# First attention units without zeros in their loads: keys between zeros that lie on chip, eight buffers instead of four

## The chip, the cores and the metric

One Trainium2 chip, and of it one core. A core has five engines that run their own instruction streams and wait for each other by semaphores: PE (matrix products, with a queue of its own for weight loads, PEld), DVE (vector work), ACT (activations and copies), POOL (vector work on SBUF alone) and SP, which in this kernel issues almost all transfers between memory and SBUF. Sixteen DMA engines carry the transfers out. The metric is the time of one execution in microseconds (us), the median over runs.

## The reference

Attention in chunks of 32 queries, each of which sees 8 memory keys and a window of the sequence (16 keys to the left, its own 32, 8 to the right), and then a layer of two matrix products with a leaky bend between them:

```python
batch, n_heads, seq, head_dim = (4, 8, 768, 64)
chunk, left_ctx, right_ctx = (32, 16, 8)
...
    k_full = np.concatenate([mem_k, k_ctx], axis=2)
    v_full = np.concatenate([mem_v, v_ctx], axis=2)
    scores = scale * np.matmul(q_c, k_full.transpose(0, 1, 3, 2))
    scores = scores - np.max(scores, axis=-1, keepdims=True)
    a = np.exp(scores)
    a = a / (np.sum(a, axis=-1, keepdims=True) + 1e-09)
    out[:, :, c_start:c_end] = np.matmul(a, v_full)
...
h = x @ w_in                                          # 3072 x 512 by 512 x 2048
g = np.maximum(h, 0.0) + alpha * np.minimum(h, 0.0)
return (g @ w_out)                                    # 2048 x 512
```

All is 32-bit floating point. The two weight matrices reach the kernel as 64-bit words and are decoded on the chip into a high and a low part, so that each product of the layer is three products in PE's faster 32-bit form.

## The kernel before

The attention is cut into 32 units: half a sequence (384 queries) of a pair of heads. Four units (the four pairs of a half) give one block of 384 columns of the layer's input. The layer runs over blocks and over 16 slices `f` of the hidden width: `up` (L723) makes `h_ps` from the input's high and low parts (`xh`, `xl`) and `w_in`, ACT and DVE bend it (L732, L735) and split it, `down` (L753) adds it up in `o_ps` with `w_out`.

The first eight units (`NWIN`, two blocks) go another way than the later 24, since PE has nothing else to do until their results are there. A unit of this kind is loaded by `load_first` (L486) into a buffer `early` that borrows the place of a weight slice: `NSET` = 4 such buffers, in the places of the last four slices. It holds queries, keys and values of a pair of heads. The 128 rows of queries and keys are 64 of one head and 64 of the other. So that one product over all 128 rows gives the scores of both heads apart, the queries come from memory with zeros: for each chunk of 32 queries 64 columns, 32 with the first head's rows filled and 32 with the second's. That is `NQ` = 768 columns for 384 queries, and 656 KB for queries and keys. The values, 256 KB, come in a second load.

`windows` (L496) then runs a unit through this chain:
- PE: `score_products` (L300), twelve products of 64 weight columns by 64 keys (L312). Before those of the first three units stand `stir` products (L298) of the tile `busy`, whose result nobody uses, 8, 2 and 2 of them (`STIR`).
- DVE: `top` (L505 or L507 hide keys outside the sequence, L509 takes the maximum), `less` (L513); ACT: `exps` (L517); DVE: `total` (L521), `inverse` (L524); POOL: `scale` (L534, L538) into `ew`, spread so that a transpose puts every key in its own row.
- PE: `turn` (L546, six transposes); ACT: `keep` (L551, two copies); PE: `values` (L559); ACT and DVE: `split` (L474, L477) into `xh` and `xl`.

Two buffers each serve the scores in PSUM, `e`, `ew` and the turned weights. A weight slice passes through ACT and DVE too (`decode_part`: L622, L630, L634, L638, L646, L649).

The order of all engines is written by a planner, `Plan`: each step has an engine, an assumed cost, what it reads and writes and when it is due. It fills the engines as a list scheduler would, with the step that has the longest way behind it first; `SHIFT` corrects that number for single steps, and `LAND` is the time it assumes from the end of a load's sending to its landing. The instructions then stand in that order in each engine's stream, and each engine runs its stream strictly in order. SP too: a load that must wait for its buffer holds up every load behind it.

Of the kernel before, what the change touches and what calls it, by code (L numbers as in the profile page):

```python
# [72 lines left out]
HOP, LAND, FOLLOW = 0.07, 2.3, 0.1  # L73
# [29 lines left out]
STIR = (8, 2, 0, 0)  # L103
# [78 lines left out]
def body(ctx: ExitStack, tc: tile.TileContext, qvw, kw, first, w_in, w_out, alpha, out):  # L182
# [22 lines left out]
    nc.vector.memset(busy, 1.0)  # L205
# [94 lines left out]
    def score_products(u):  # L300
# [6 lines left out]
        q = t[:, :NQ].rearrange("p (c x) -> p c x", c=NT * NJ)  # L307
        keys = t[:, NQ:NQ + NT * NKT].rearrange("p (t k) -> p t k", t=NT)
        for n in range(2 * NJ):
            for i in range(2):  # L310
                t, j = n // NJ * 2 + i, n % NJ
                nc.tensor.matmul(  # L312
                    out=st["s"][i * 2 * CH:(i + 1) * 2 * CH, n],
                    lhsT=q[:, t * NJ + j],
                    rhs=keys[:, t, STARTS_WIN[j]:STARTS_WIN[j] + KW],
                    start=True, stop=True,
                )
# [167 lines left out]
    def load_first(u):  # L485
        blk, pr = divmod(u, NPAIR)  # L486
        t = early[u % NSET]

        def load(lo, hi):
            nc.sync.dma_start(out=t[:, lo:hi], in_=first[blk, pr, :, lo:hi])  # L490
# [4 lines left out]

    def windows(u):  # L496
# [5 lines left out]
        def top():  # L502
            s = st["s"]
            if u // NPAIR % 2 == 0:
                nc.vector.memset(s[0:2 * CH, 0, 0:LEFT], NEG)  # L505
            else:
                nc.vector.memset(s[2 * CH:4 * CH, 2 * NJ - 1, KW - NM - RIGHT:KW - NM], NEG)  # L507
# [450 lines left out]
```

## Time and profile before

| | us |
|---|---|
| median of three runs | 598.39 (598.30 to 599.01) |
| the profiled execution | 598.74 |
| its span, first to last instruction | 596.8 |
| PE busy | 588.1 (99%) |
| DVE busy | 387.1 (65%) |
| ACT busy | 210.9 (35%) |
| POOL busy | 37.9 (6%) |
| DMA engines, mean busy share in the first ten of 40 slices | 0.8, 0.9 or more three times, 0.6, 0, 0, 0.2, 0.2, 0.2 |

The granted TensorE clock is 1.00 throughout. In an order of time a row gives the start and the duration in us, the engine, the line of the kernel, the operation, output<-input with their shapes, the count, and in brackets how long the engine had stood idle and for whom. In a table of groups the two numbers behind the bar are busy us and mean ns of one, then the idle us before them. `SPq` is SP's stream of transfers. In a table of waits the three numbers are us in total, times, and the longest.

### The profile page before, as it was taken

To read this page: it belongs to the slowest core of one execution; us is meant where nothing else is said; L and a number is where in the kernel's file an instruction comes from. 1 tells how busy PE (TensorE), PEld (TensorE's weight loads), DVE (VectorE), ACT (ScalarE), POOL (GpSimd) and SP (SyncE) were. 2 spreads that over 40 slices of the span, in tenths; PEclk is the share of its full clock that TensorE was granted. 3 is DMA by queue.
4 is the path that set the end of the run, shared out by engine and by line. 5 is a ranking of instruction groups with operands and counts; after the bars stand their busy time and mean duration, and the time that the engine had idled before them with its cause. 6 is when DMAs were issued, how large, how long until landed. Compare 5 with 4: busy or idle time off the path is not lost.

```text
span 596.8 us, 10948 instructions
## 1 busy us (share of the span) xinstructions
PE 588.1 (99%) x4412; PEld 504.9 (85%) x4412; DVE 387.1 (65%) x904; ACT 210.9 (35%) x580; POOL 37.9 (6%) x61
## 2 busy tenths in 40 slices
PE   7999999999999999999999999999999999999997
PEld 4789989888998989989898888888888888888886
DVE  5888889887958768695895852861862771530530
ACT  3788887635122504423233302302400411210201
POOL 3510000010001101010010100100100100000000
PEclk9999999999999999999999999999999999999999
DMA  8999600222040312503304003003101000000001
GB/s 328 351 400 407 246 0 1 66 65 89 2 153 2 100 33 69 152 3 100 100 1 154 1 1 100 2 0 112 60 1 36 0 1 36 36 1 0 1 1 70
DMA packets 21075, 48.95 MB, mean 82 GB/s; under 512 B 2464, under 2 KB 5792, under 8 KB 21024
## 3 DMA queue, kind: packets, MB, share of 16 engines
q1 hardware_dynamic: 20880, 48.12, 22.8%
q8 instruction: 34, 0.56, 0.4%
q14 instruction: 17, 0.14, 0.1%
q10 hardware_dynamic: 144, 0.13, 0.1%
HBM read 41.95 MB, written 6.29 MB: 81 GB/s over the span
## 4 chain that ended last, share of the span: by engine, by line
PE 96%; DMA 3%; SPq 0%; ACT 0%; issue 0%; ACTq 0%
PE h_ps L723 45%; PE o_ps L753 44%; PE a_ps L438 3%; DMA early<-first 3%; PE s_ps L337 2%; PE a_ps L559 1%; PE o_ps L546 0%; PE s_ps L312 0%; SPq L490 0%; SPq L599 0%; ACT o_t L810 0%; ACTq L810 0%
## 5 line engine op out<-in xcount | busy, mean ns | idle before, releaser
L723 PE MATMUL h_ps<-xh,w 128*128 128x384 f32 (+1 forms) x896 | 248.7, 358 | 0.0
L723 PEld LDWEIGHTS h_ps<-xh,w 128*128 128x128 f32 x896 | 164.9, 188 | 16.0
L753 PE MATMUL o_ps<-w,gh 128*128 128x512 f32 x528 | 162.7, 389 | 0.0
L723 PE MATMUL h_ps<-xl,w 128*128 128x384 f32 (+1 forms) x448 | 162.6, 363 | 0.0
L732 ACT ACTIVATE g<-h_ps 128x384 f32<-128x384 f32 (+1 forms) x112 | 60.4, 540 | 195.3 <-PE h_ps L723 129.8
L735 DVE SCALAR_TENSOR_TENSOR g<-g,rise,h_ps 128x384 f32<-128x384 f32 (+1 forms) x112 | 74.7, 668 | 74.8 <-ACT g L732 74.1
L753 PEld LDWEIGHTS o_ps<-w,gh 128*128 128x128 f32 x528 | 99.1, 188 | 20.5
L413 DVE STREAM_TRANSPOSE pt<-e 32x64 f32<-32x64 f32 (+1 forms) x336 | 99.3, 300 | 7.4 <-POOL e L392 2.0
L753 PE MATMUL o_ps<-w,gl 128*128 128x512 f32 x264 | 102.8, 389 | 0.0
L723 PEld LDWEIGHTS h_ps<-xl,w 128*128 128x128 f32 x448 | 84.1, 188 | 10.2
L753 PE MATMUL o_ps<-w,xh 128*128 128x512 f32 x240 | 74.8, 393 | 0.0
L753 PEld LDWEIGHTS o_ps<-w,gl 128*128 128x128 f32 x264 | 49.6, 188 | 10.2
L477 DVE TENSOR_TENSOR xl<-a_ps,xh 128x384 fp32r<-128x384 f32 x32 | 17.6, 552 | 59.7 <-ACT xh L474 59.0
L753 PEld LDWEIGHTS o_ps<-w,xh 128*128 128x128 f32 x240 | 45.0, 188 | 8.9
L392 POOL TENSOR_TENSOR e<-e,den 128x384 f32<-128x384 f32 x24 | 22.8, 948 | 419.6 <-DVE den L389 270.0
L474 ACT CAST xh<-a_ps 128x384 fp32r<-128x384 f32 x32 | 15.0, 482 | 95.5 <-PE a_ps L438 93.7
L741 DVE CAST gh<-g 128x512 fp32r<-128x512 f32 (+1 forms) x72 | 28.8, 401 | 30.6 <-PE o_ps L753 28.2
L745 DVE TENSOR_TENSOR gl<-g,gh 128x512 fp32r<-128x512 f32 (+1 forms) x72 | 46.6, 648 | 1.7
L371 ACT ACTIVATE e<-s_ps,mx 128x64 f32<-128x64 f32 x144 | 43.4, 318 | 11.0 <-DVE mx L363 11.0
L753 PE MATMUL o_ps<-w,xl 128*128 128x512 f32 x120 | 46.8, 390 | 0.0
L371 ACT ACTIVATION_READ_ACCUMULATOR e<-s_ps,mx 128x1 f32 x144 | 30.4, 211 | 0.0
L810 ACT COPY o_t<-o_ps 128x512 f32<-128x512 f32 x21 | 12.2, 591 | 44.6 <-PE o_ps L753 44.2
(57 smaller groups left out, 376.4 us busy)
## 6 DMA issues: line engine op xcount, KB each, us to landing
w_t<-w_in SPq DMA_DIRECT2D x16, 512.0 KB, 10.2
w_t<-w_out SPq DMA_DIRECT2D x16, 512.0 KB, 10.2
qk<-kw SPq DMA_DIRECT2D x24, 272.0 KB, 4.2
v_t<-qvw SPq DMA_DIRECT2D x24, 256.0 KB, 2.8
out<-o_t SPq DMA_DIRECT2D x23, 256.0 KB, 2.1
early<-first SPq DMA_DIRECT2D x8, 656.0 KB, 7.2
qk<-qvw SPq DMA_DIRECT2D x24, 192.0 KB, 4.5
early<-first SPq DMA_DIRECT2D x8, 256.0 KB, 7.1
```

Source lines behind the costliest of these rows:

```text
L371: nc.scalar.activation(out=st["e"][:, i], in_=st["s"][h2][:, n], func=AF.Exp, scale=SCALE, bias=d["mx"][:, u - us[0], n, h2:h2 + 1], accum ...
L392: nc.gpsimd.tensor_tensor(out=st["e"], in0=st["e"], in1=st["den"].broadcast_to([P, NJ * 2, KW]), op=ALU.mult)
L413: nc.vector.transpose(out=pts[u % NPT][quad * CH:(quad + 1) * CH, j, t0:t0 + n1 - n0].rearrange("p t h q -> p (t h) q"), in_=(st["e"], zer ...
L438: nc.tensor.matmul(out=st["a"][h2 * D:(h2 + 1) * D, t * TQ:(t + 1) * TQ], lhsT=st["v"][:, t, h2, :], rhs=pts[u % NPT][:, :, t, h2, :], sta ...
L474: nc.scalar.copy(out=ring[k][0][:, cols], in_=st["a"][:, :BT])
L477: nc.vector.tensor_tensor(out=ring[k][1][:, cols], in0=st["a"][:, :BT], in1=ring[k][0][:, cols].bitcast(F32), op=ALU.subtract)
L723: nc.tensor.matmul(out=h["ps"][:, :n_cols], lhsT=ws[f, 0][:, wk, k * P:(k + 1) * P], rhs=parts(blk, k)[1](xk), start=(k == 0 and n == 0), ...
L732: nc.scalar.activation(out=h["g"], in_=h["ps"][:, :n_cols], func=AF.Relu, scale=-1.0)
L735: nc.vector.scalar_tensor_tensor(out=h["g"], in0=h["g"], scalar=rise[:, f:f + 1], in1=h["ps"][:, :n_cols], op0=ALU.mult, op1=ALU.add)
L741: copy(out=h["gh"], in_=h["g"])
L745: nc.vector.tensor_tensor(out=h["gl"], in0=h["g"], in1=h["gh"].bitcast(F32), op=ALU.subtract)
L753: nc.tensor.matmul(out=o_ps[tt], lhsT=h[gk][:, tt * P:(tt + 1) * P], rhs=ws[f, 1][:, wk], start=(f == first_f and i == 0), stop=(f == last ...
```

## The change

Queries now come without zeros (384 columns instead of 768), in one load with the values (`first`, 896 columns), except for unit 0, whose values come in a load of their own. The zeros lie among the keys instead, and are written on the chip: `early` has room for the keys twice, for the first head and for the second, and all of it is cleared at the start, the first head's part by POOL and the second's by DVE. Each head's keys are then loaded into their own part and their own rows. For this the rows of the two heads alternate (row 2d is the first head's dimension d, row 2d+1 the second's), and a load of keys goes to every other row, 64 of 128, from a new input `keys`. A score product takes 32 queries as weights and the keys of both heads, 2 x 64, as columns; the score tile's rows are now the four tiles of 96 queries and its columns chunk and head, which the steps behind follow. There are eight buffers instead of four, so none is used twice. `busy` is written by POOL after its first zeros instead of by DVE, 7 `stir` products stand before the first unit instead of 8, and `LAND` and the table `SHIFT` have other numbers, so that the planner's order moves.

```diff
-HOP, LAND, FOLLOW = 0.07, 2.3, 0.1
+HOP, LAND, FOLLOW = 0.07, 3.1, 0.1
...
-STIR = (8, 2, 0, 0)
+STIR = (7, 2, 0, 0)
...
-NWIN, NSET = 2 * NPAIR, 4
+NWIN, NSET = 2 * NPAIR, 8
...
-    nc.vector.memset(busy, 1.0)
+    early = [wps[NF - NSET + i, 0].tile([P, BT + 2 * NKEYS + NV], F32, name="early", tag="w") for i in range(NSET)]
+    for i, t in enumerate(early):
+        for h2 in range(2):
+            (nc.gpsimd, nc.vector)[h2].memset(t[:, h2 * NKEYS:(h2 + 1) * NKEYS], 0.0)
+        if i == 0:
+            nc.gpsimd.memset(busy, 1.0)
...
-        for n in range(2 * NJ):
-            for i in range(2):
-                t, j = n // NJ * 2 + i, n % NJ
+        for j in range(NJ):
+            for t4 in range(NT):
                 nc.tensor.matmul(
-                    out=st["s"][i * 2 * CH:(i + 1) * 2 * CH, n],
-                    lhsT=q[:, t * NJ + j],
-                    rhs=keys[:, t, STARTS_WIN[j]:STARTS_WIN[j] + KW],
+                    out=st["s"][t4 * CH:(t4 + 1) * CH, 2 * j:2 * j + 2],
+                    lhsT=q[:, t4 * NJ + j],
+                    rhs=ks[:, t4, :, STARTS_WIN[j]:STARTS_WIN[j] + KW],
                     start=True, stop=True,
                 )
...
-        step(SP, 1.6, partial(load, 0, NQ + NT * NKT), writes=[("qk", u % NSET)], rest=due(u))
-        step(SP, 0.78, partial(load, NQ + NT * NKT, NQ + NT * NKT + NV), writes=[("fv", u % NSET)], rest=due(u))
+        for h2 in range(2):
+            rows = slice(h2, P, 2)
+            step(SP, 0.35, partial(load, keys[blk, pr, rows], h2 * NKEYS, rows), writes=[("fk", u % NSET, h2)],
+                 rest=due(u))
+        if u == 0:
+            step(SP, 0.52, partial(load, first[blk, pr, :, :BT], 2 * NKEYS), writes=[("fq", u % NSET)], rest=due(u))
+            step(SP, 0.67, partial(load, first[blk, pr, :, BT:BT + NV], 2 * NKEYS + BT), writes=[("fv", u % NSET)],
+                 rest=due(u))
+        else:
+            step(SP, 1.13, partial(load, first[blk, pr, :, :BT + NV], 2 * NKEYS),
+                 writes=[("fq", u % NSET), ("fv", u % NSET)], rest=due(u))
```

SP's stream from its start, before. `early_157` to `early_160` are the four buffers; 1312 columns are queries and keys, 512 are values, and `w_t` is a weight slice on its way in.

```order
L490 DMA early_157<-first 128x1312
L490 DMA early_158<-first 128x1312
L490 DMA early_159<-first 128x1312
L490 DMA early_160<-first 128x1312
L599 DMA w_t_228<-w_in 128x1024
L490 DMA early_158<-first 128x1312
L490 DMA early_157<-first 128x1312
L490 DMA early_157<-first 128x512
L490 DMA early_158<-first 128x512
L490 DMA early_160<-first 128x1312
L599 DMA w_t_346<-w_out 128x1024
L490 DMA early_159<-first 128x1312
```

The same place now, with buffers 153 to 160; 384 columns are queries, 896 queries and values, and each key row stands for the two halves.

```order
L493 DMA early_153<-first 128x384
L493 DMA early_153<-keys 64x544 x2
L493 DMA early_154<-first 128x896
L493 DMA early_154<-keys 64x544 x2
L493 DMA early_155<-first 128x896
L493 DMA early_155<-keys 64x544 x2
L493 DMA early_156<-first 128x896
L493 DMA early_156<-keys 64x544 x2
L493 DMA early_157<-first 128x896
L493 DMA early_157<-keys 64x544 x2
L493 DMA early_153<-first 128x512
L493 DMA early_158<-first 128x896
```

Then follow the second half of `early_158`'s keys, the first `w_in`, and the last two units. Five units come before the first values alone, and the first weight slice has moved from the fifth load to the twentieth.

DVE's stream from its start, before: `busy` and `warm`, then the first unit's `top` and `less`.

```order
L205 MEMSET busy 128x512
L224 MEMSET warm 128x1
L505 MEMSET s_ps 64x16
L509 TENSOR_REDUCE mx<-s_ps 128x6
L513 TENSOR_TENSOR e<-s_ps,mx 128x6x64
```

And now:

```order
L208 MEMSET early 128x544 x8
L228 MEMSET warm 128x1
L517 MEMSET s_ps 32x2x16
L521 TENSOR_REDUCE mx<-s_ps 128x6
L525 TENSOR_TENSOR e<-s_ps,mx 128x6x64
```

Eight clearings of 544 columns stand where one memset of `busy` stood.

ACT's stream from its start, before: the exponentials of units 0 and 1 (L517), the first weight slice (L622), and the copies of turned weights (L551).

```order
L225 ACT_TABLE_LOAD
L225 ACTIVATE warm<-warm 128x1
L517 ACTIVATE e<-e 128x6x64 x2
L622 ACTIVATE a<-w_t 128x512
L551 COPY qk_154<-o_ps 128x384 x2
L517 ACTIVATE e<-e 128x6x64 x2
```

And now, with L529 for the exponentials and L563 for the copies:

```order
L229 ACT_TABLE_LOAD
L229 ACTIVATE warm<-warm 128x1
L529 ACTIVATE e<-e 128x6x64 x2
L563 COPY qk_178<-o_ps 128x384
L529 ACTIVATE e<-e 128x6x64
L563 COPY qk_178<-o_ps 128x384
```

The weight slice is gone from this place, and unit 2's exponentials stand behind one copy instead of two.

More of the change, by code (lines that the diff above doesn't have):

```diff
@@ L181, in body @@
 @with_exitstack
-def body(ctx: ExitStack, tc: tile.TileContext, qvw, kw, first, w_in, w_out, alpha, out):
+def body(ctx: ExitStack, tc: tile.TileContext, qvw, kw, first, keys, w_in, w_out, alpha, out):
     nc = tc.nc
@@ L487, in load_first, with load @@
         t = early[u % NSET]
-        def load(lo, hi):
-            nc.sync.dma_start(out=t[:, lo:hi], in_=first[blk, pr, :, lo:hi])
+        def load(x, lo, rows=slice(0, P)):
+            nc.sync.dma_start(out=t[rows, lo:lo + x.shape[-1]], in_=x)
         state[u] = {}
-        step(SP, 1.6, partial(load, 0, NQ + NT * NKT), writes=[("qk", u % NSET)], rest=due(u))
-        step(SP, 0.78, partial(load, NQ + NT * NKT, NQ + NT * NKT + NV), writes=[("fv", u % NSET)], rest=due(u))
+        for h2 in range(2):
[9 more added lines that the diff above has]
+                 writes=[("fq", u % NSET), ("fv", u % NSET)], rest=due(u))
     def windows(u):
@@ L543, in turn, with keep @@
             stir(st["t"][0], STIR[3])
-            for t in range(2):
+            for h2 in range(2):
                 for j in range(NJ):
-                    nc.tensor.transpose(st["t"][t][:, j * P:(j + 1) * P], ews[u % NPT][:, t, j], eye)
-        def keep(t):
-            et = qk[u % NKB][:, :2 * NJ * P].rearrange("p (t x) -> p t x", t=2)
-            st["et"] = et.rearrange("p t (j a h q) -> p t j a h q", j=NJ, a=2, h=2)
-            nc.scalar.copy(out=et[:, t], in_=st["t"][t][:, :NJ * P])
+                    nc.tensor.transpose(st["t"][h2][:, j * P:(j + 1) * P], ews[u % NPT][:, h2, j], eye)
+        def keep(h2):
+            et = qk[u % NKB][:, :2 * NJ * P].rearrange("p (h x) -> p h x", h=2)
+            st["et"] = et.rearrange("p h (j t q) -> p h j t q", j=NJ, t=NT)
+            nc.scalar.copy(out=et[:, h2], in_=st["t"][h2][:, :NJ * P])
         def values():
@@ L555, in values @@
             st["a"] = pool.tile([P, 512], F32, name="a_ps", tag=tag)
-            v = early[u % NSET][:, NQ + NT * NKT:].rearrange("p (t h d) -> p t h d", t=NT, h=2)
+            v = early[u % NSET][:, BT + 2 * NKEYS:BT + 2 * NKEYS + NV].rearrange("p (t h d) -> p t h d", t=NT, h=2)
             for t in range(NT):
@@ L601, in load_w @@
         i = f - NF + NSET
-        after = [("qk", i), ("fv", i)] if i >= 0 else []
+        after = [("fk", i, 0), ("fk", i, 1), ("fq", i), ("fv", i)] if i >= 0 else []
         for i in range(2):
@@ L904, in body @@
     plan.send()
-_ORDER = ["qvw", "kw", "first", "w_in", "w_out", "alpha"]
+_ORDER = ["qvw", "kw", "first", "keys", "w_in", "w_out", "alpha"]
 def _layout(q, k, v, mem_k, mem_v, moe_w_in, moe_w_out, moe_alpha):
```

38 lines of the change are left out of this document (18 added, 20 removed).

## The prediction

> **What bounds the kernel now.** I read the page first, then the chain of waits, then the order of time on PE, and only then DVE and the loads. The page says how little there is to win:
>
> ```profile
> span 596.8 us, 10948 instructions
> PE 588.1 (99%) x4412; PEld 504.9 (85%) x4412; DVE 387.1 (65%) x904; ACT 210.9 (35%) x580; POOL 37.9 (6%) x61
> ```
>
> PE lacks 596.8 - 588.1 = 8.7 us of being busy throughout, and a part of the 588.1 is no work (the products of `busy`). The chain of waits, in order of time (start, duration, what), says where the 8.7 us lie:
>
> ```profile
> 2.11 7.87 DMA early<-first
> ...
> 10.11 0.93 PE s_ps L312 x24
> ...
> 12.21 9.57 DMA early<-first
> ...
> 21.83 0.92 PE s_ps L312 x24
> ...
> 24.21 0.81 PE a_ps L559 x16
> ...
> 571.38 21.77 PE o_ps L753 x96
> 593.15 0.03 ACTq L810
> ```
>
> Until 21.83 the end hangs on loads of `early`; after that every piece up to 593.15 is PE's, without a gap. So an edit in the first 22 us moves the end by what it saves there, and no edit of a load can save anything later. The order of time on PE (start, duration, what, and in brackets the idle time before it and who ended it) shows the stage:
>
> ```profile
> 1.46 3.59 PE L298 MATMUL s_ps<-busy 128*128 128x512 bf16 x8 [1.46 <-DVE warm L224]
> 4.98 1.40 PE L312 MATMUL s_ps<-early 128*64 128x64 f32 x24
> ...
> 10.11 0.92 PE L312 MATMUL s_ps<-early 128*64 128x64 f32 x24 [0.83 <-DMA early<-first]
> ...
> 12.70 0.44 PE L546 MATMUL o_ps<-eye,ew 128*128 128x128 f32 x2 [0.87 <-POOL ew L534]
> 13.62 0.66 PE L546 MATMUL o_ps<-eye,ew 128*128 128x128 f32 x4 [0.48 <-POOL ew L538]
> ...
> 15.91 0.92 PE L312 MATMUL s_ps<-early 128*64 128x64 f32 x24 [0.67 <-DMA early<-first]
> ...
> 19.44 1.16 PE L546 MATMUL o_ps<-eye,ew 128*128 128x128 f32 x6 [0.34 <-POOL ew L534]
> 21.83 0.92 PE L312 MATMUL s_ps<-early 128*64 128x64 f32 x24 [0.23 <-DMA early<-first]
> ...
> 24.95 0.44 PE L723 MATMUL h_ps<-xl,w 128*128 128x384 f32 x1
> ```
>
> The first score products start when the eight products of `busy` are through (1.46 + 3.59 = 5.05). From then on PE waits three times for a load (0.83 + 0.67 + 0.23 = 1.73 us) and three times for POOL's scaled weights (0.87 + 0.48 + 0.34 = 1.69 us): 3.4 us in all. Whether the first sum can simply be taken away depends on the engine between the two, DVE:
>
> ```profile
> 6.00:22.00 16.00, 12.39 (x220) 9.20 (x219) 13.15 (x35) 8.88 (x20) 6.33 (x14) 1.00 1.02 389
> ```
>
> In this stretch (busy time of PE, PEld, DVE, ACT, POOL, then the granted clock, the share of the DMA engines and GB/s) DVE works 13.15 of 16.0 us, and the DMA engines are full at 389 GB/s. DVE, not PE, is the next limit. Its own order of time tells what it lost to late loads:
>
> ```profile
> 0.91 0.48 DVE L205 MEMSET busy<- 128x512 bf16 x1 [0.91 <-PEq L949]
> ...
> 6.46 0.07 DVE L505 MEMSET s_ps<- 64x16 f32 x1 [5.06 <-PE s_ps L312]
> ...
> 11.10 0.07 DVE L505 MEMSET s_ps<- 64x16 f32 x1 [0.43 <-PE s_ps L312]
> ...
> 16.92 0.07 DVE L507 MEMSET s_ps<- 64x8 f32 x1 [1.23 <-PE s_ps L312]
> ...
> 22.83 0.07 DVE L507 MEMSET s_ps<- 64x8 f32 x1 [0.30 <-PE s_ps L312]
> ```
>
> After its start DVE stood still 0.43 + 1.23 + 0.30 = 1.96 us because score products were late, and those were late for the loads named above.
>
> **Part 1: the loads.** The DMA table gives sizes (count, KB each, median us to landing):
>
> ```profile
> qk<-kw SPq DMA_DIRECT2D x24, 272.0 KB, 4.2
> early<-first SPq DMA_DIRECT2D x8, 656.0 KB, 7.2
> early<-first SPq DMA_DIRECT2D x8, 256.0 KB, 7.1
> ```
>
> A unit took 656 + 256 = 912 KB and now takes 192 (queries) + 256 (values) + 272 (keys in two halves) = 720 KB; eight units save 1536 KB, 1.57 MB, which at 389 GB/s is 4.0 us of a full queue. That is not the gain, since the order changes too. By SP's rows the score products of unit n need, in KB sent before and with them, 464, 1184, 1904, 2624, 3344, then 4320 (unit 0's values come between), 5552 (the first `w_in` too) and 6272. The fourth unit's 2624 KB are exactly the four loads of 656 KB that it needed before, so it comes no earlier than 10.11 again and the first of the three waits stays. From there 720 KB take 1.90 us: units 4 to 7 arrive at 12.0, 14.6, 17.8 and 19.7. PE waited for unit 4 until 15.91 and for the last one until 21.83, so the second and third wait go. Eight buffers also take these waits from SP:
>
> ```profile
> SPq L490 <- PE o_ps L546: 2.8, 3, 1.3
> SPq L490 <- PE s_ps L312: 2.4, 2, 1.4
> ```
>
> Loads of units 4 to 7 stood 5.2 us until PE had read a buffer, and every later load stood behind them. SP issues 25 loads where it issued 16; at 0.5 us each (1.98 for four, quoted below) that is 4.5 us more of SP's time, hidden because the DMA engines are full.
>
> No row shows a load of 64 rows. It takes at best half of a 128-row load of the same rows (`qk<-kw`) and at worst as long as it; I take half, since every other load in the trace runs at the rate of a full queue, and carry the other end to the rivals. [...]
>
> **Part 2: the zeros.** DVE now clears eight pieces of 128x544 ahead of everything, POOL eight more and then `busy` after its first. POOL's price is near at hand, and so is what waits for it:
>
> ```profile
> 0.74 1.98 SPq L490 DMA_DIRECT2D early<-first  x4
> ...
> 0.73 0.20 POOL L214 MEMSET eye<- 128x128 f32 x1 [0.29 <-POOLq L949]
> ...
> 1.32 1.41 POOL L222 MEMSET ew<- 128x768 f32 x2
> ...
> 9.72 0.62 POOL L534 TENSOR_TENSOR ew<-e,den 128x256 f32<-128x256 f32 x1 [6.99 <-DVE s_ps L505]
> ```
>
> 0.70 us for 768 elements is 0.50 for 544. POOL starts at 0.73, so its first piece is done at 1.23, `busy` at 1.7, all its zeros and the 2 us of older memsets before 8, and the first scaling came at 9.72 in this execution. The first key load stands in SP behind piece 0 (1.23) and the second behind DVE's (1.5), with the query load ahead of them at 0.74: no loss that the products of `busy` don't cover, as seven of them from about 1.75 at 0.45 us each end at 4.9, where eight ended at 5.05. DVE's piece is not in the trace: by elements, L205's 0.48 for 512 gives 0.51; by bytes, with four for each element against two, 1.02. Eight end at 5.0 or at 9.1. A row of DVE on 4-byte elements,
>
> ```profile
> L509 DVE TENSOR_REDUCE mx<-s_ps 128x6 f32<-128x384 f32 x8 | 4.5, 558 | 0.3
> ```
>
> lies between: 0.558 for 384 is 0.79 for 544, an end at 7.2, but it reads PSUM and reduces as well. I take 0.6 and an end near 5.7, by the memset. That lies under the 5.06 us that DVE idled before 6.46; beyond it each microsecond would delay all of DVE's queue. [...]
>
> **Part 3: the score products.** Twelve of 64 weight columns by 64 keys become twelve of 32 by 128.
>
> ```profile
> L337 PE MATMUL s_ps<-qk 64*32 64x64 f32 x1152 | 14.9, 224 | 0.0
> L312 PE MATMUL s_ps<-early 128*64 128x64 f32 x192 | 7.8, 235 | 1.8 <-DMA early<-first 1.7
> ...
> 110.66 1.17 PE s_ps L337 x82
> ```
>
> Twice the columns stream, over four groups of 32 columns where two of 64 were. L337 shows that narrow groups overlap: 1152 rows in 12 pairs of units are 96, and a pair takes 1.17 us, 12 ns each, against 0.92 / 24 = 38 ns at L312. If four overlap the price stays 0.92; if only two do, the streaming, 0.92 less the 0.235 that one row lasts, doubles: 0.69 us more. I take the first. Transposes, value products and copies keep their shapes.
>
> **Part 4: what now paces the start.** With the later loads there, DVE gives back 1.23 + 0.30 = 1.53 us of its idle time; the 0.43 stays with the fourth unit. PE's own two waits are only 0.90 of it, the rest reaches PE through POOL. Against it stands a new place to wait: DVE's sum for unit 2 used to stand behind `w_in`'s copy (L630); now only two short steps part it from that unit's subtraction, while on ACT the exponentials between the two are still behind a copy of unit 0's transposes, which are no earlier than before:
>
> ```profile
> 11.45 0.66 ACT L622 ACTIVATE a<-w_t 128x512 f32<-128x512 f32 x1 [1.45 <-DMA w_t<-w_in]
> 12.02 0.85 ACT L551 COPY qk<-o_ps 128x384 f32<-128x384 f32 x2
> ```
>
> Behind that sum DVE holds the fifth unit's maximum. The price is one copy, 0.43 us, less what overlaps: 0.3. The first row shows when the first `w_in` was there: 11.45. It is now SP's 20th load instead of the fifth and lands near 16; DVE's four steps on it then fall among the last units, and the first product at L723 came only at 24.95. The later weights come up to 4 us earlier, which nobody waits for. **Sum:** -1.53 (DVE's waits) - 0.15 (shorter start) + 0.3 = -1.4 us. The profiled execution took 598.74 (1.9 around its span) and would take 597.3; it stands 0.35 over the median of 598.39, so I forecast a median of 597.0. Ends: all of PE's 3.4 us gone, 595.0; nothing gained, 598.4.
>
> **Rivals.**
> (a) The waits only change their names. PE's 1.69 us behind POOL show that the ring PE, DVE, ACT, DVE, POOL, PE with two buffers is tight already; if it holds each unit back, half or less of the 1.4 is left: 597.7 to 598.4. For it speaks DVE's 13.15 of 16.0; against it that 1.23 of its idle time is one single late load.
> (b) Half loads at half speed. Keys would take 0.72 us more for each unit; the last arrives at 19.7 + 5.8 = 25.5 instead of 21.83, 3.7 us late, while PE does some 1.5 us of transposes and values that used to follow: +2.2, 600.6, slower. It decides once a half load runs at less than about 0.7 of the full rate, where the lateness eats the 1.4. Against it: rows alternate, so each half touches all the partitions that a full load does.
> (c) Narrow products overlap only two at a time: 8 x 0.69 = 5.5 us more on PE, of which its idle time (16.00 - 12.39 = 3.6, less the 1.4) hides 2.2: +3.3 - 1.4 = +1.9, 600.3. L337 speaks against it.
> (d) All waits go, POOL's too, as units arrive ahead of need: 595.0. DVE's share speaks against it.
>
> **How the numbers follow.** Chances: forecast 0.51 (its own range 596.1 to 597.6), (a) 0.27, (b) 0.07, (c) 0.08, (d) 0.07. A measurement tells about 0.2%, 1.2 us, from no change: under 597.2 counts as faster, over 599.6 as slower. Faster: (d) and 0.44 of the forecast, 0.51. Same: the rest of the forecast, (a), and 0.02 of a milder (c), 0.36. Slower: 0.13. The forecast and (a) hold 0.78, so the range reaches a little way towards (d) and a milder (c): 595.3 to 599.2.
>
> **What would show it.** In the profile after: one PE wait on `early` of under 0.9 us near 10 and none after 12; DVE's memsets at 0.5 to 0.65 us each and its first maximum at 6.3 to 6.7; the last score products before 20.5 and the first L736 before 23.5; score products of a warm unit at 0.8 to 1.0 us; from about 31 us the chain pure PE. Memsets past 6.5, key halves that land over 2 us apart, or score products of 1.5 us would make the forecast wrong at parts 2, 1 and 3, and a new PE wait after 31 us at the claim that nothing later moves.

## The result, and the profile after

The changed kernel is slower: 600.6 us (median of seven runs, 599.82 to 602.04) against 598.41 for the kernel before on the same chip (seven runs, 598.01 to 599.01), a ratio of 1.0027 with a 95% interval of 1.0014 to 1.004. Executions over 1.5% longer than the fastest of the same kernel (four in all the runs below, of 975 to 2058 us) are left out of every ratio. The profiled execution took 600.17, its span is 598.4. From the page:

```profile
span 598.4 us, 10989 instructions
PE 587.2 (98%) x4411; PEld 503.5 (84%) x4411; DVE 390.8 (65%) x911; ACT 210.5 (35%) x580; POOL 40.0 (7%) x70
```

PE is busy 0.9 us less and stands idle 11.2 us instead of 8.7. The order of time on PE says where (its rows of score products, and the first product of the layer):

```profile
4.90 1.51 PE L315 MATMUL s_ps<-early 128*32 128x128 f32 x24
...
8.66 0.86 PE L315 MATMUL s_ps<-early 128*32 128x128 f32 x24 [1.71 <-DMA early<-keys]
...
10.44 0.86 PE L315 MATMUL s_ps<-early 128*32 128x128 f32 x24 [0.38 <-DMA early<-keys]
12.30 0.86 PE L315 MATMUL s_ps<-early 128*32 128x128 f32 x24 [0.99 <-DMA early<-keys]
...
14.50 0.86 PE L315 MATMUL s_ps<-early 128*32 128x128 f32 x24 [0.53 <-DVE den L536]
...
17.31 0.86 PE L315 MATMUL s_ps<-early 128*32 128x128 f32 x24 [0.25 <-DMA early<-keys]
...
21.55 0.93 PE L315 MATMUL s_ps<-early 128*32 128x128 f32 x24 [1.76 <-DVE e L525]
...
25.45 0.42 PE L736 MATMUL h_ps<-xl,w 128*128 128x384 f32 x1
```

Unit 3 has its keys at 12.30 where it had them at 10.11, and PE waits 3.33 us for keys instead of 1.73 for loads. No wait of PE for POOL's weights is left in this time, but 0.53 and 1.76 us for DVE have come. The first L736 starts at 25.45 instead of 24.95. Busy time in stretches of 2 us (columns as in the prediction, the last three are the granted clock, the share of the DMA engines and GB/s), after:

```profile
2.00:4.00 2.00, 2.00 (x6) 0.70 (x5) 1.75 (x5) 0.01 (x1) 2.00 (x5) 1.00 0.77 230
4.00:6.00 2.00, 2.00 (x27) 1.05 (x25) 1.33 (x4) 0.20 (x1) 1.93 (x8) 1.00 0.83 250
6.00:8.00 2.00, 0.95 (x10) 0.11 (x2) 1.20 (x3) 0.18 (x1) 1.10 (x2) 1.00 0.82 274
8.00:10.00 2.00, 1.34 (x26) 0.74 (x26) 0.35 (x2) 0.34 (x1) 0.00 (x0) 1.00 0.98 339
```

and the same stretches before, with the one behind them:

```profile
2.00:4.00 2.00, 2.00 (x7) 0.60 (x6) 0.00 (x0) 0.22 (x2) 0.73 (x2) 1.00 0.88 320
4.00:6.00 2.00, 2.00 (x23) 1.16 (x22) 0.00 (x0) 0.00 (x0) 0.00 (x0) 1.00 1.01 407
6.00:8.00 2.00, 1.99 (x37) 1.24 (x36) 1.31 (x5) 0.25 (x1) 0.00 (x0) 1.00 1.01 412
8.00:10.00 2.00, 1.28 (x26) 0.78 (x24) 1.97 (x6) 0.80 (x2) 0.28 (x1) 1.00 1.06 412
10.00:12.00 2.00, 1.72 (x30) 1.45 (x30) 1.53 (x6) 0.55 (x1) 0.84 (x3) 1.00 0.95 278
```

From 2 to 10 us the loads run at 230 to 339 GB/s where they ran at 320 to 412; from 10 us on the rate is near the old one (374 to 396 from 10 to 20 us, against 394 to 418 from 12 to 20 before). From 2 to 10 us they move 2 x (230 + 250 + 274 + 339) KB = 2.2 MB, against 3.1 MB before. Idle engines are only a part of it: 250 GB/s at a share of 0.83 is 301 for a full share, where 407 at 1.01 is 403, so the engines also moved less while they were at work. The second loss is further on; these are the orders of time on ACT and on DVE, after:

```profile
19.62 0.66 ACT L635 ACTIVATE a<-w_t 128x512 f32<-128x512 f32 x1 [1.55 <-DMA w_t<-w_in]
20.19 0.46 ACT L563 COPY qk<-o_ps 128x384 f32<-128x384 f32 x1
```

```profile
0.92 4.53 DVE L208 MEMSET early<- 128x544 f32 x8 [0.92 <-PEq L962]
...
6.51 0.09 DVE L517 MEMSET s_ps<- 32x32 f32 x1 [1.05 <-PE s_ps L315]
...
20.32 0.75 DVE L643 COPY w_t<-w_t 128x512 int16<-128x512 int16 x1 [0.84 <-ACT a L635]
```

The first `w_in` lands at 19.62, ACT waits 1.55 us for it with a copy and an exponential behind it, DVE waits 0.84 for ACT, and unit 6's scores wait for DVE.

### The profile page after: what moved, and what is told of

The parts are those of the page before. It is cut to its first block, busy times and chain, and to the rows that moved or that the text cites. A ratio compares the mean times of both kernels' runs of the same rounds, so it can differ in the third digit from the quotient of the medians.

```text
span 598.4 us, 10989 instructions
## 1 busy us (share of the span) xinstructions
PE 587.2 (98%) x4411; PEld 503.5 (84%) x4411; DVE 390.8 (65%) x911; ACT 210.5 (35%) x580; POOL 40.0 (7%) x70
## 4 chain that ended last, share of the span: by engine, by line
PE 96%; DMA 2%; POOL 1%; DVE 0%; issue 0%; ACT 0%; SPq 0%; ACTq 0%; POOLq 0%
PE h_ps L736 45%; PE o_ps L766 44%; PE a_ps L441 3%; PE s_ps L340 2%; DMA w_t<-w_in 1%; PE a_ps L571 1%; DMA early<-keys 1%; POOL early L208 1%; PE o_ps L558 1%; PE s_ps L315 0%; ACT a L635 0%; DVE e L525 0%; ACT o_t L823 0%; DVE den L533 0%; POOL busy L210 0%
## 5 line engine op out<-in xcount | busy, mean ns | idle before, releaser
L736 PE MATMUL h_ps<-xh,w 128*128 128x384 f32 (+1 forms) x896 | 248.8, 359 | 0.0
L736 PEld LDWEIGHTS h_ps<-xh,w 128*128 128x128 f32 x896 | 164.8, 188 | 16.0
L736 PE MATMUL h_ps<-xl,w 128*128 128x384 f32 (+1 forms) x448 | 162.7, 363 | 0.0
L416 DVE STREAM_TRANSPOSE pt<-e 32x192 f32<-32x192 f32 (+1 forms) x336 | 99.4, 301 | 7.5 <-POOL e L395 2.0
L736 PEld LDWEIGHTS h_ps<-xl,w 128*128 128x128 f32 x448 | 84.1, 188 | 10.2
```

Source lines behind the costliest of these rows:

```text
L416: nc.vector.transpose(out=pts[u % NPT][quad * CH:(quad + 1) * CH, j, t0:t0 + n1 - n0].rearrange("p t h q -> p (t h) q"), in_=(st["e"], zer ...
L736: nc.tensor.matmul(out=h["ps"][:, :n_cols], lhsT=ws[f, 0][:, wk, k * P:(k + 1) * P], rhs=parts(blk, k)[1](xk), start=(k == 0 and n == 0), ...
```

## The experiments

All times are ratios to runs of the kernel before on the same chip, with the 95% interval. The first question is why the early loads are slow. Theory I: SP's issue, now three transfers a unit and without a pause until 17 us. H: loads of 64 rows. Z: the zeroing that runs beside them. Later S: many small transfers are slow at a queue's start, whatever else changes; N and R split it into the number of transfers and the length of their rows. B concerns the wait for the first weight.

**Zeroing alone**

```diff
+    for i in range(8):
+        nc.gpsimd.memset(qk[0][:, 384:928], 0.0)
+        nc.vector.memset(qk[1][:, 384:928], 0.0)
     eye = const.tile([P, P], F32, name="eye")
```

> The kernel before, with the sixteen zeroings of the change added alone: eight memsets of 128x544 on VectorE and eight on GpSimd, into two tiles that nothing else uses in the first 12 us; loads, order and products are those of before. If the zeroing is what slows the early loads (theory Z): in 2 to 6 us the loads move 230 to 300 GB/s instead of 320 and 407, unit 1's scores start near 8 instead of 6.84, and the time is up by 0.8 to 2 us, 599.2 to 600.4. If SP's issue (theory I) or the half loads (theory H) are the cause: 320 and 407 GB/s as before, unit 1 at 6.8 to 7.0, and 598.0 to 598.9.

Ratio 0.9995 (0.9986 to 1.0003). The stretches:

```profile
4.00:6.00 2.00, 2.00 (x28) 1.09 (x27) 1.46 (x4) 0.00 (x0) 1.81 (x6) 1.00 1.01 417
6.00:8.00 2.00, 1.34 (x26) 0.78 (x24) 1.67 (x6) 0.20 (x1) 1.48 (x5) 1.00 1.02 417
```

DVE and POOL are as busy as in the change (1.46 and 1.81 of 2 us), and the loads keep their 417 GB/s. Z falls, at least beside large transfers.

**The same number of transfers, but whole rows**

```diff
-        for h2 in range(2):
-            step(SP, 0.35, partial(load, keys[blk, pr, rows], h2 * NKEYS, rows), ...)
+        whole = [(keys[blk, pr], 0), (first[blk, pr, :, :BT], 2 * NKEYS)]      # units 1 to 7
+        for h2 in range(2):
+            step(SP, 0.35, partial(load, *whole[h2]), ...)
...
-            step(SP, 1.13, partial(load, first[blk, pr, :, :BT + NV], 2 * NKEYS), ...)
+            step(SP, 1.13, partial(load, first[blk, pr, :, BT:BT + NV], 2 * NKEYS + BT), ...)
```

> The changed kernel, with a unit's 720 KB still in three transfers from unit 1 on, but all of 128 rows: the values, both heads' keys in one (into the first head's part, so that the scores are not the reference's: each head's keys lie in the wrong place), and the queries. Unit 0 is loaded as in the change. SP's issue theory (I): three issues of 0.58 us a unit as before this edit, units 1 to 3 within 0.3 us of 8.66, 10.44 and 12.30, time 600.3 to 600.9. Half loads (H): the loads move about 400 GB/s from 4 us on, units 1 to 3 near 7.6, 9.4 and 11.2, time 598.8 to 599.8. Zeroing (Z): 230 to 280 GB/s in 2 to 6 us as in the change and unit 1 within 0.3 us of 8.66; later units may gain where the zeroing has ended; 600.0 to 600.9.

Ratio 1.0017 (1.0008 to 1.0027).

```profile
4.00:6.00 2.00, 2.00 (x27) 1.06 (x25) 1.33 (x4) 0.20 (x1) 1.93 (x8) 1.00 0.86 261
6.00:8.00 2.00, 0.82 (x10) 0.11 (x2) 1.20 (x3) 0.30 (x1) 1.10 (x2) 1.00 0.91 270
```

The loads are as slow as in the change, with no half row among them but unit 0's: H falls for the units behind it. Unit 0's two halves still open the queue here; that the loads are slow without any half row is shown by `before_split` below. Against I speaks SP's order of time in this run (the second row holds unit 1's last transfer and unit 2's first),

```profile
3.16 0.43 SPq L493 DMA_DIRECT2D early<-keys  x1
3.63 0.91 SPq L493 DMA_DIRECT2D early<-first  x2
```

1.34 us for a unit's three transfers, where the change takes 0.58 + 1.11 = 1.69:

```profile
2.53 0.58 SPq L493 DMA_DIRECT2D early<-first  x1
3.16 1.11 SPq L493 DMA_DIRECT2D early<-keys  x2
```

SP is quicker and the loads are not. By its issue time alone SP would have supplied 720 KB in 1.34 us, 550 GB/s, twice what moved.

**Half of the keys by ACT's queue.** Two tries; the second puts the memset that ACT's first activation reads ahead of the zeroing and gives ACT units 0 to 3 only.

```diff
-            nc.sync.dma_start(out=t[rows, lo:lo + x.shape[-1]], in_=x)
+            queue.dma_start(out=t[rows, lo:lo + x.shape[-1]], in_=x)    # second half: nc.scalar
```

> The changed kernel, with the second head's eight key halves sent by ACT's queue instead of SP's; nothing else moves. I: SP has two issues a unit, some 1.2 us instead of 1.78, so it gets ahead of the DMA engines; units 1 to 3 sooner by 0.6 to 1.1 us (7.6 to 8.1, 9.4 to 9.8, 11.2 to 11.7) and 599.0 to 600.0. H and Z: units 1 to 3 within 0.3 us of the change's 8.66, 10.44 and 12.30; ACT spends eight issues of about 0.55 us between its exps and copies, and the time is 600.4 to 601.8.

Ratio 1.0155 (1.0138 to 1.0172), a fault of the experiment: ACT's first activation stood behind DVE's zeroing until 5.51 us and the halves behind it; the first scores started at 11.49.

> The run with halves on ACT's queue again, mended: there ACT's first activation waited for VectorE's zeroings until 5.51 us and the halves were sent behind it. Here the memset it reads stands ahead of the zeroings, and ACT sends the second head's halves of units 0 to 3 alone. I: units 1 to 3 sooner by 0.6 to 1.1 us (7.6 to 8.1, 9.4 to 9.8, 11.2 to 11.7), 599.0 to 600.0. S and Z2: SP's issue is not what holds them, units 1 to 3 within 0.3 us of 8.66, 10.44 and 12.30, 600.2 to 601.

Ratio 1.0011 (1.0003 to 1.002). Units 1 to 3 start at 8.17, 10.20 and 11.71, sooner by 0.49, 0.24 and 0.59: less than I asks for and a little more than its rivals grant. But the median, 599.48, lies in the range that I gave, and the loads run faster than the change's 250 and 274 GB/s:

```profile
4.00:6.00 2.00, 1.54 (x24) 0.66 (x25) 1.35 (x3) 0.00 (x0) 1.93 (x8) 1.00 0.99 343
6.00:8.00 2.00, 0.82 (x14) 0.13 (x5) 1.20 (x3) 0.32 (x1) 1.10 (x2) 1.00 0.92 310
```

A third try gives ACT all six halves of units 1 to 3:

> The changed kernel, whole and with the reference's result, with the six key halves of units 1 to 3 sent by ACT's queue (ACT's first activation stands ahead of the zeroings). If two queues side by side hide what each transfer costs at the start: 330 to 400 GB/s in 4 to 8 us, units 1 to 3 at 7.6 to 8.0, 9.5 to 10 and 11.3 to 11.7, time 598.6 to 599.5. If the stretch is one of the engines and not of the queue: units 1 to 3 within 0.3 us of the 8.17, 10.20 and 11.71 of four halves by ACT and 599.3 to 600.

Ratio 1.0018 (1.0006 to 1.003), with 266 and 360 GB/s in the same stretches and unit 1 at 9.28 in the profiled execution: no more than four halves did. A second queue took back a part of the loss in one run and less in the other, so the way the transfers are issued may own a part of it; the intervals don't settle how much.

**Without the zeroing**

```diff
-            (nc.gpsimd, nc.vector)[h2].memset(t[:, h2 * NKEYS:(h2 + 1) * NKEYS], 0.0)
...
-partial(load, keys[blk, pr, rows], h2 * NKEYS, rows)
+partial(load, keys[blk, pr, rows], 0, rows)
...
-                    rhs=ks[:, t4, :, STARTS_WIN[j]:STARTS_WIN[j] + KW],
+                    rhs=ks[:, t4, 0:1, STARTS_WIN[j]:STARTS_WIN[j] + KW].broadcast_to([P, 2, KW]),
```

> The changed kernel with its loads as they are (three a unit, the same 64-row halves), but without the sixteen zeroings: both heads' halves go into one key part, whose rows they fill together, and the products read that part for both heads, so the scores are not the reference's. Theory Z2 (zeroing beside transfers of many small packets slows them): 2 to 8 us move 330 to 400 GB/s instead of 230, 250 and 274, units 1 to 3 near 7.3, 9.1 and 10.9, time 598.6 to 599.8. Theory S (small packets and many transfers are slow at the start by themselves): 220 to 290 GB/s in 2 to 8 us, units 1 to 3 within 0.3 us of 8.66, 10.44 and 12.30, time 600.2 to 601.

Ratio 1.0021 (1.0012 to 1.0031).

```profile
4.00:6.00 2.00, 2.00 (x28) 0.87 (x26) 0.39 (x2) 0.00 (x0) 0.00 (x0) 1.00 0.92 297
6.00:8.00 2.00, 0.02 (x1) 0.00 (x0) 0.81 (x2) 0.52 (x1) 0.00 (x0) 1.00 0.82 259
```

Little DVE (0.39 and 0.81 of 2 us) and no POOL beside the loads, and still 297 and 259 GB/s, the first a little above the range that S gave and both below Z2's. So Z2 falls as the main cause, and S is left; that the zeroing owns a small part, 297 against 250, is not ruled out. The starts of the units are not compared: after a pause of 2.76 us PE's clock fell to 0.50 between 8 and 9 us.

**One transfer a unit**

```diff
-            step(SP, 1.13, partial(load, first[blk, pr, :, :BT + NV], 2 * NKEYS), ...)
+            step(SP, 1.13, partial(load, first[blk, pr], NKEYS), ...)     # keys of both heads, queries, values
```

> The changed kernel with its sixteen zeroings, but a unit's 720 KB from unit 1 on in one transfer of 128 rows of 5760 B (keys of both heads, queries and values side by side; the keys lie in one part, so the scores are not the reference's). S: 380 to 415 GB/s from 4 us on as before the change, units 1 to 3 near 7.0, 8.8 and 10.6, time 598.2 to 599.4. Z2: the zeroing still slows them, 230 to 300 GB/s until about 7 us, units 1 to 3 near 8.3, 10.1 and 11.9, time 599.8 to 600.6.

Ratio 1.0016 (1.0007 to 1.0025). Units 1 to 3 start at 8.68, 10.44 and 12.17, where S had put them near 7.0, 8.8 and 10.6, but the stretches change in the middle:

```profile
4.00:6.00 2.00, 2.00 (x27) 1.05 (x25) 1.33 (x4) 0.20 (x1) 1.93 (x8) 1.00 0.81 262
6.00:8.00 2.00, 1.16 (x10) 0.13 (x2) 1.20 (x3) 0.19 (x1) 1.10 (x2) 1.00 0.98 369
```

The median, 599.49, is just above the range that S gave too. Unit 0's three small transfers open the queue here as in the change, and until 6 us it is as slow. So unit 0 went the same way:

> The run with one 720 KB transfer a unit, now for unit 0 too (its three first transfers of 192 and 2 times 136 KB fall away; the scores are again not the reference's). S, with the slow stretch at the start of a queue's work and not in the kernel's units: after a first transfer of some 2.5 us every later one takes 1.9 us, units 0 to 3 at 5.2, 7.1, 9.0 and 10.9, and 598.0 to 599.2. If the slow stretch comes with the change itself (its input, its tiles, its zeroing): 240 to 270 GB/s until 6 us again, unit 1 near 8.7, 599.2 to 600.2.

```profile
4.00:6.00 2.00, 1.08 (x8) 0.23 (x10) 1.33 (x4) 0.20 (x1) 1.93 (x8) 1.00 0.99 395
6.00:8.00 2.00, 1.70 (x42) 1.04 (x41) 1.11 (x3) 0.00 (x0) 1.11 (x2) 1.00 1.01 400
```

Ratio 0.9992 (0.9983 to 1.0001), units 1 to 3 at 7.57, 9.33 and 11.38, with all the zeroing in place. The slow stretch is gone, and with it the loss; unit 0's halves are gone too, so this run alone doesn't part them from the number. The gain that the prediction saw in it is not there either, though unit 0's load begins 0.7 us late, behind DVE's first zeroing.

**Small transfers in the kernel before.** The reverse: only the cut is added, three transfers of 128 rows for the same 656 KB.

```diff
-            nc.sync.dma_start(out=t[:, lo:hi], in_=first[blk, pr, :, lo:hi])
+            cuts = [lo, 448, 880, hi] if lo == 0 else [lo, hi]
+            for a, b in zip(cuts, cuts[1:]):
+                nc.sync.dma_start(out=t[:, a:b], in_=first[blk, pr, :, a:b])
```

> The kernel before with each unit's 656 KB load cut by columns into three transfers of 128 rows (1792, 1728 and 1728 B a row); bytes, tiles, buffers and order are unchanged and nothing is zeroed. S (several small transfers a unit make the first 8 us of loads slow, whatever else changes): 240 to 330 GB/s in 4 to 8 us instead of 407 and 412, unit 1 at 7.3 to 8.5 instead of 6.84, unit 3 at 10.8 to 12, time 599.0 to 600.6. If not S (what slows the change is in its other parts): 380 to 412 GB/s, unit 1 at 6.8 to 7.1, 598.2 to 599.0.

```profile
4.00:6.00 2.00, 1.07 (x7) 0.42 (x7) 0.00 (x0) 0.00 (x0) 0.00 (x0) 1.00 0.80 250
6.00:8.00 2.00, 1.77 (x30) 1.12 (x32) 1.03 (x3) 0.00 (x0) 0.00 (x0) 1.00 0.98 326
```

Ratio 1.0023 (1.0014 to 1.0033): the change's slow stretch and nearly its whole loss, from the cut alone, with no half row and no zeroing. S holds.

**Number or row length.** `before_pieces` keeps one transfer and cuts the rows; `before_rows` and `before_rows16` cut into three transfers and keep the rows whole.

```diff
-            nc.sync.dma_start(out=t[:, lo:hi], in_=first[blk, pr, :, lo:hi])
...
+            nc.sync.dma_start(out=t[:, :hi].rearrange("p (c x) -> p c x", c=4),      # before_pieces
+                              in_=first[blk, pr, :, :4 * 344].rearrange("p (c x) -> p c x", c=4)[:, :, :328])
...
+            cuts = [0, 43, 86, P] if lo == 0 else [0, P]     # before_rows; before_rows16: [0, 48, 96, P]
+            for a, b in zip(cuts, cuts[1:]):
+                nc.sync.dma_start(out=t[a:b, lo:hi], in_=first[blk, pr, a:b, lo:hi])
```

> The kernel before with each unit's 656 KB in one transfer, but every row of 5248 B in four pieces of 1312 B, which lie 64 B apart in the input. R: 240 to 330 GB/s in 4 to 8 us, unit 3 near 11 to 12, time 599.4 to 601. N: 380 to 415 GB/s, unit 3 near 10.1, 598.3 to 599.1.

```profile
4.00:6.00 2.00, 2.00 (x27) 1.13 (x25) 0.00 (x0) 0.00 (x0) 0.00 (x0) 1.00 1.06 394
6.00:8.00 2.00, 1.97 (x32) 1.01 (x28) 1.48 (x5) 0.52 (x1) 0.00 (x0) 1.00 1.07 375
```

Ratio 1.0014 (1.0005 to 1.0023). Rows of 1312 B cost 3% and 9% of the rate in these two stretches, not 39% and 21% as the cut into three did; the slow start is not theirs. But the median, 599.55, lies in the range that R gave: short rows have a price of their own, 0.14%, and here it is paid later too (367 to 389 GB/s from 12 to 20 us, 394 to 418 before). So a part of the cut's 0.23% may be its rows' and not its number's.

> The kernel before with each unit's 656 KB load cut into three transfers by rows (43, 43 and 42 rows of 5248 B) instead of by columns. If the number of transfers is what slows the start (theory N): 240 to 330 GB/s in 4 to 8 us as with the cut by columns (250 and 326), unit 3 near 11.7, time 599.6 to 600.8. If it is their short rows (theory R): 380 to 415 GB/s, unit 3 near 10.1 and 598.3 to 599.1.

> The kernel before with each unit's 656 KB load cut by rows again, now into 48, 48 and 32 rows of 5248 B. N (the number of transfers): 240 to 340 GB/s in 4 to 8 us, unit 3 between 10.8 and 12, time 599.2 to 600.8. If only transfers of short rows are slow in number, or the number does nothing where rows are whole: 380 to 415 GB/s, unit 3 near 10.1, 598.3 to 599.1.

Neither could answer. Ratio 1.2289 (1.2272 to 1.2305) for 43 rows, where the share of this row stands in every stretch from 4 to 22 us, at 24 to 26 GB/s:

```profile
8.00:10.00 2.00, 0.00 (x0) 0.00 (x0) 0.00 (x0) 0.00 (x0) 0.00 (x0) 0.74 0.06 26
```

A share of 0.06 is one sixteenth: what one DMA engine of the sixteen would give, though it does not tell how many worked. And 1.0232 (1.0218 to 1.0247) for 48, 48 and 32 rows:

```profile
4.00:6.00 2.00, 1.18 (x7) 0.30 (x7) 0.00 (x0) 0.00 (x0) 0.00 (x0) 1.00 1.08 218
...
10.00:12.00 2.00, 1.14 (x13) 0.55 (x12) 1.42 (x4) 0.00 (x0) 0.00 (x0) 0.50 1.07 220
```

The engines' share is 0.97 to 1.08 from 4 to 14 us, at 217 to 226 GB/s where the kernel before moved 403 to 412 but for the dip to 278: half the rate, and not only at the start. These bands of rows have a price of their own, so the number of transfers with whole rows was not isolated this way. The last run sets the change between three transfers and one:

```diff
+            part = partial(load, keys[blk, pr], 0) if h2 == 0 else lambda: None
-            step(SP, 0.35, partial(load, keys[blk, pr, rows], h2 * NKEYS, rows), ...)
+            step(SP, 0.35, part, ...)
```

> The changed kernel with both heads' keys of a unit in one transfer of 128 rows (into the first head's part, so the scores are not the reference's), and queries with values in the other: 720 KB in two transfers instead of three, zeroing and all else as in the change. N: between three transfers a unit (250 to 261 and 270 to 274 GB/s in 4 to 6 and 6 to 8 us, unit 3 at 12.2 to 12.3) and one from unit 0 on (395 and 400, unit 3's keys in time): 270 to 340 GB/s in 4 to 8 us, unit 1 at 7.6 to 8.4, time 598.9 to 600.0. If not N: units 1 to 3 within 0.3 us of 8.66, 10.44 and 12.30, and 600.2 to 601.

Ratio 1.0005 (0.9996 to 1.0014), inside the range that N gave. In its profiled execution, of 975 us, the granted clock fell to 0.56 between 6 and 8 us and stayed there, so only the loads are read: 321 GB/s in 4 to 6 us and 318 in 6 to 8, between the three transfers and the one. One transfer fewer a unit took back most of the change's loss. It is not the number alone that differs: the halves are gone as well, unit 0's too, and against three transfers of whole rows (1.0017, 1.0008 to 1.0027) the intervals overlap. The number of transfers is the reading that fits all these runs; none isolates it.

**The wait for the first weight**

```diff
+MOVE = ((178, 69), (179, 103), (180, 179))     # step n goes behind step m
...
```

> The changed kernel, with the first weight's three decode steps moved back in their engines' rows: ACT's L635 behind two copies, an exps and a cast, DVE's L643 and L647 behind unit 5's subtraction and unit 4's sum. Theory B (the wait of ACT for the first weight, which stands ahead of unit 4's copy and exps, is what keeps PE idle for 1.76 us before unit 6's scores): the wait goes below 0.6 us and the time falls by 0.7 to 1.5 us, to 599.1 to 599.9. Rival (the loads of units 6 and 7 are late themselves, last packets at 20.07 and 22.71 us): PE then waits for the keys until about 20.9 and 23.5, the gain is under 0.6 us and the time 600.0 to 600.8.

Ratio 1.0032 (1.0021 to 1.0043). The order of time on PE:

```profile
7.96 1.51 PE L324 MATMUL s_ps<-early 128*32 128x128 f32 x24 [1.81 <-DMA early<-keys]
...
21.47 1.45 PE L324 MATMUL s_ps<-early 128*32 128x128 f32 x24 [1.82 <-DMA early<-keys]
```

The wait before unit 6 is as long as it was, and now it has the keys' name. B falls as a cause: the place of the weight in ACT's row only hid that unit 6's keys were late as well. The change's own trace agrees: SP issued these keys there from 13.86 us on, and a half took about 7.2 us to land, so they were there at 21.1 at the earliest, against a start at 21.55.

**Eight buffers alone.** In the first try the planner's table named other steps, since eight units' loads now come first; in the second the table is carried over, but for one entry, which in the new numbers names another step, and one value, 4.5, which became 5.7.

```diff
-NWIN, NSET = 2 * NPAIR, 4
+NWIN, NSET = 2 * NPAIR, 8
```

> The kernel before with eight buffers instead of four, alone; its planner, which no longer waits for buffers, sends six units' loads of 656 KB in a row and the first weight as the twelfth transfer. Prediction's step on eight buffers (SP never waits for a buffer; the loads of before from 12 us on lose their gap): 412 GB/s without the dip to 278 in 10 to 12 us, unit 3 at 9.9 to 10.1, unit 4 by 12.2, time 597.0 to 598.2. Rival (the first weight comes later, and ACT and DVE wait for it in the middle of the units' work): PE loses 1 to 2 us near 18 to 22 us, time 598.8 to 600.5.

Ratio 1.0016 (1.0007 to 1.0024), a median of 599.78, in the range that the rival gave. ACT waits for the weight as the rival says, but PE's long waits stand ahead of it and have the loads' name (the first two rows are PE's):

```profile
9.72 0.92 PE L312 MATMUL s_ps<-early 128*64 128x64 f32 x24 [1.80 <-DMA early<-first]
...
18.20 1.11 PE L559 MATMUL a_ps<-qk,early 128*64 128x96 f32 x16 [2.01 <-DMA early<-first]
...
19.49 0.67 ACT L622 ACTIVATE a<-w_t 128x512 f32<-128x512 f32 x1 [2.24 <-DMA w_t<-w_in]
```

For the weight's decoding PE waits 0.92 us, at 27.77. So the rival had the price, and the moved order of the units' loads most of the cause.

> The kernel before with eight buffers, and its table of shifts carried over to the new step numbers, so that the first twelve transfers keep the order of before, the first weight fifth. With the earlier run on eight buffers the table's numbers named other steps, unit 5 was loaded third and the first weight as the eleventh. Eight buffers as a gain: no dip to 278 GB/s in 10 to 12 us, the loads of units 4 to 7 land 0.7 to 2 us sooner, PE's waits after 12 us go down by 0.5 to 1 us, and the time is 597.2 to 598.2. Rival: PE there waits on POOL and DVE and not on the loads, 598.2 to 599.0.

```profile
10.00:12.00 2.00, 1.64 (x30) 1.33 (x30) 1.37 (x5) 0.94 (x3) 0.65 (x3) 1.00 1.02 407
```

Ratio 0.9988 (0.9978 to 0.9998), 598.26 against 598.77: the dip to 278 GB/s is gone and the kernel a little faster. The median lies just inside the range that the rival gave, and as it says most of PE's waits after the start are for DVE, ACT and POOL (2.9 us in sum, against 1.1 for loads).

**Fewer bytes in one transfer.** What the change aimed at, without the cut: the queries travel without zeros beside the keys, and two copies a unit spread them into a tile that was zeroed once.

```diff
+    apart = [wps[NF - NSET - NAP + i, 0].tile([P, NQ], F32, name="apart", tag="w") for i in range(NAP)]
+    for i, t in enumerate(apart):
+        (nc.vector, nc.gpsimd)[i % 2].memset(t, 0.0)
...
-        step(SP, 1.6, partial(load, 0, NQ + NT * NKT), writes=[("qk", u % NSET)], rest=due(u))
+        step(SP, 1.13, partial(load, 0, BT + NT * NKT), writes=[("qk", u % NSET)], rest=due(u))
...
+        def spread(h2):
+            rows = slice(h2 * D, (h2 + 1) * D)
+            q = apart[u % NAP][rows].rearrange("p (c h q) -> p c h q", h=2, q=CH)[:, :, h2]
+            (nc.scalar.copy, nc.gpsimd.tensor_copy)[h2](out=q, in_=early[u % NSET][rows, :BT].rearrange("p (c q) -> p c q", q=CH))
```

> The kernel before with eight buffers (its table carried over), whose queries come without their zeros: 464 KB of queries and keys a unit in one transfer of 128 rows instead of 656 KB, and two copies a unit, of 64 rows by ACT and of 64 rows by GpSimd, spread them into one of four tiles that are zeroed once at the start. The result is the reference's. If fewer bytes pay once a unit stays one transfer: 370 to 412 GB/s from 4 us on, units 1 to 3 near 6.3, 7.4 and 8.8, all of PE's waits after 12 us under 2.5 us in sum, time 596.8 to 598.0. Rival (the copies stand in ACT's and GpSimd's rows ahead of the exps and products of other units, and PE waits for these instead): PE loses 1 us or more on ACT or POOL in 8 to 22 us, time 598.3 to 599.5.

Ratio 0.9987 (0.9977 to 0.9996), 598.05 against 598.78. The waits of PE in this run (us in total, times, longest):

```profile
PE s_ps L302 <- DVE busy L206: 1.5, 1, 1.5
PE o_ps L550 <- POOL ew L542: 1.4, 3, 0.5
PE s_ps L316 <- POOL apart L573: 0.8, 1, 0.8
PE s_ps L316 <- DVE s_ps L509: 0.8, 1, 0.8
```

No load is among them. The median lies between the ranges of the two expectations. Units 1 to 3 start at 6.55, 8.13 and 9.80, later than expected, and the first L734 at 21.77, 3.2 us ahead of the L723 of before, of which 0.7 us reach the end. For POOL and DVE hold PE for 3.0 us after its first wait, nearly the 3.4 of before. This kernel and the one with eight buffers are faster than the kernel before, by 0.13% and 0.12%; between these two no difference is shown.

## Why the prediction was wrong

The forecast was 597.0 us, faster or the same, with a range of 595.3 to 599.2; 600.6 lies outside it.

The step that failed is in part 1: "from there 720 KB take 1.90 us", a rate of 389 GB/s carried over from loads of 656 KB to loads cut in three, with nothing for the cut. It measured 230 to 274 GB/s from 2 to 8 us and 339 from 8 to 10; unit 3, put at 10.11, came at 12.30. With it fell the sentence that SP's longer issue is "hidden because the DMA engines are full": their share was 0.77 to 0.83. The cut alone, put into the kernel before, slows the loads in the same way and costs 0.23% where the change loses 0.27%, and a single transfer a unit takes the loss away; that is shown. Why several small transfers are slow at a queue's start, and from about 10 us on hardly are (384 GB/s in the change, 406 in the cut kernel before from 10 to 12), stays open: neither SP's issue time nor short rows account for the slow start by themselves, though each may own a part, and what the engines do in the share that they stand idle was not seen.

Rival (b), half loads at half speed, had the right time, 600.6, by luck, and the wrong mechanism: without half rows after unit 0 the loads were as slow (261 and 270 GB/s in 4 to 8 us of `three_whole`, 250 and 274 in the change). What the prediction holds against it is wrong as well: a half lands on 64 of the 128 partitions, every other one, and not on all. That a half takes half the time of a full load was the prediction's estimate, and its 1.90 us, 720 KB over 389 GB/s, has no price for one more transfer; no run shows a half alone. What was measured is that one load for the keys of both heads instead of two halves (`two_whole`) brought 1.0027 to 1.0005.

Part 4 failed twice. `w_in`, put "near 16", landed at 19.62, since every load ahead of it was late; but the wait behind it (1.76 us on PE) would have been one for keys otherwise. And the -1.4 us was too large even with the loads in time: one load a unit is at 0.9992, and `compact`, where no unit waits for a load, gains 0.13%, some 0.7 us. There rival (a) was right: PE's waits took POOL's and DVE's name, 3.0 us of them. The clearing of unit 0's keys ahead of its load, which part 2 let pass as no loss, did cost nothing in the change, where queries and the first half keep SP busy.

Part 2 was right in its numbers: DVE's eight memsets follow each other every 0.57 us and end at 5.45 (0.6 and 5.7 forecast), the first maximum comes at 6.63, POOL's pieces follow every 0.50. The price went by elements: one of the eight lasts 0.51 us on average for 544 elements of four bytes, 0.94 ns each, as did L205 before, 0.48 us for 512 of two bytes; by bytes it would have been 1.02 us. Part 3 was right: the score products behind unit 0's take 0.86 to 0.93 us, against 0.92 before, so four groups overlap, and rival (c) falls. That nothing after the start moves held as well: from 21.55 us to 594.61 every piece of the chain of waits is PE's, and what the first units lost, the end loses.

## What to carry to other kernels

Price a transfer's place in time, not only its bytes: from 4 to 8 us of this kernel three transfers of a third were 39% and 21% slower than one (`before_split`), so to save bytes by cutting a load can cost more than the bytes. A form that leaves one transfer of all 128 rows, and expands on other engines, lost nothing here (`compact`), but no gain over eight buffers alone is shown for it. And when loads come sooner, look for the next ring in the chain first: here POOL and DVE kept most of what the loads gave back.

## What the runs showed of the hardware that was not expected

With 43 and 42 rows the loads ran at 24 to 26 GB/s and a share of 0.06 from 4 to 22 us (`before_rows`), and no row here shows loads of 43 and of 42 rows apart. Bands of 48 and 32 neighbouring rows had a share of 0.97 to 1.08 (`before_rows16`) and still moved only 217 to 226 GB/s from 4 to 14 us, while the change, with halves of every other row among its loads, moved 396 from 12 to 14 us:

```profile
12.00:14.00 2.00, 1.67 (x30) 1.26 (x30) 1.25 (x5) 0.33 (x1) 0.62 (x3) 1.00 1.03 396
```

Why these bands move so little was not shown.

To issue a half of every other row keeps SP no shorter than to issue a load of all 128 rows: 0.47 to 0.59 us (median 0.50) in the change, against 0.33 to 0.59 in `three_whole` (medians 0.36 and 0.43). Two halves thus cost SP 1.11 us where one load at the same place took 0.43.

PE's clock fell after some short pauses and not after others. In `decode_moved` PE paused 1.81 us, and then:

```profile
8.00:10.00 2.00, 2.00 (x26) 1.14 (x26) 0.41 (x2) 0.00 (x0) 0.00 (x0) 0.50 1.01 384
```

That is half of the clock, for 3 us, with score products of 1.51 us instead of 0.86. In `before_rows16` a pause of 1.59 us did the same (0.50 from 9 us on, score products of 1.55 us instead of 0.92):

```profile
8.92 1.55 PE L312 MATMUL s_ps<-early 128*64 128x64 f32 x24 [1.59 <-DMA early<-first]
```

In `before_eight` a pause of 1.80 us, shown above, left the clock at 1.00, as pauses of 1.71 and 1.76 us did in the profiled execution of the change. So in these traces the length of one pause alone does not decide it; what does was not shown.

The change's seven runs differ in their mean granted clock: 1.000 went with 599.82 and 599.96 us, 0.999 with 600.17, 0.997 with 600.6 to 600.94, 0.993 with 602.04. Some 0.7 us of the median's loss may therefore be the clock's. That the late loads set it off is likely but not shown: only one of these executions was traced, and the kernel before has such executions too (600.21 us at 0.994 among the runs beside `before_rows`).
